# A planner that also places the end pieces of blocks 0 to 3, with block 0's attention first alone

## The chip, the cores and the metric

The program runs on one core of one Trainium2 chip. The metric is the device time of one execution in microseconds, less is better. The kernel before takes 2083.66 us (median of 3 runs, 2082.87 to 2084.57). The engines are named as in the profile: PE (TensorE) with PEld for its weight loads, DVE (VectorE), ACT (ScalarE), POOL (GpSimd) and SP (SyncE, which issues nearly all the DMAs).

## The reference, cut to what matters

Three layers run one after the other on 2304 tokens of width 512: attention with keys and values averaged over groups of 8, a gated layer with 1536 hidden units, and a layer of 8 experts whose mixture matrix is balanced over all tokens in 8 rounds.

```
k_p, v_p = mean over 8 neighbouring rows of k, v          # 576 -> 72 rows
attn = softmax(scale * q @ k_p.T);  x = attn @ v_p        # 4 batches, 8 heads
x2 = (sigmoid(x @ w_gate) * (x @ w_val)) @ w_out          # 512 -> 1536 -> 512
P = exp(x2 @ w_gate2 - max); 8 times: P /= row sums, P /= column sums, P *= N/E
out = sum over e of P[:, e] * (relu(x2 @ w1[e]) @ w2[e])
```

Everything is fp32. A product of the second and third layer is computed as three matmuls on words that were split into a high and a low half (fp32r): high times high, high times low, low times high.

## The kernel before, in words

The tokens are cut into six blocks of 384 (NBLK, numbered 0 to 5), a block into three tiles of 128. The first two layers are done block by block; the experts come afterwards, two blocks (a pair) at a time, from L1157 to the end, and the change doesn't touch them.

Attention of a block j (attend, L925): four k pieces are loaded and summed over 8 on DVE (L266), the v rows are summed on PE by a matmul with a 0/1 matrix (spread_v, L287, batches 0 and 1) or on DVE (L276). For each of three tiles and two head groups, four matmuls give the scores (L309), DVE takes the maxima (L334, or L327 with a subtraction on L328), ACT takes the exponentials, DVE divides by the sum (L359 to L362), PE turns the result (L370, four transposes), ACT copies it, PE multiplies with v (values, L384), ACT rounds the high half of x (L396) and DVE subtracts for the low half (L400). The constant DIRECT says for which blocks ACT takes the exponentials straight from PSUM (j below it), and for which DVE subtracts the maximum first and ACT takes all exponentials at once (L352).

Gated layer: one step is one block and one slice of 128 hidden units. It has the gate product G and the value product V (L226, 12 matmuls of 128x384 each), a sigmoid on ACT (L1028), a multiplication on DVE (L1031), the high half on ACT (L1035), the low half on DVE (L1038), and the output product X (L509). The list steps1 (L107) says in which order steps of blocks 0, 1 and 2 alternate. Weights arrive as 64-bit words and have to be narrowed and split by DVE and ACT before a product can use them (chunk, L843: L162 to L178 and L200 on DVE, L153 and L196 on ACT); a slice has three such chunks.

The order of all this up to the start of block 5 comes from a planner (Plan, L419). Every task has an engine, a key, an assumed duration, the tasks it depends on, and the buffers (room) it takes and frees. The planner plays the engines forward; on each engine the ready task with the lowest key goes next, and the order in which it emits the instructions is the order on the engines' queues, which then wait on semaphores.

A block that has all its 12 slices needs its end pieces (after_block, L560): x2 is split into a high half (ACT, L548) and a low half (L549, a subtraction on POOL for blocks 0 to 4, 128x768), the halves are multiplied with the gate of the experts (12 small matmuls at L226 into "at"), the result is copied (L577), turned (L586) and copied into logits (L589), and the halves are stored. After the second block of a pair there are four more combinations of the two blocks (tt, L599 to L608), each split and stored too. In the planner all this is one generator: from the end of a block on, twelve tasks of the PE queue each run it to its next yield (L1077 to L1083). The planner knows of them only the PE time of the twelve tasks; what they put on ACT, POOL, DVE and SP, and the buffers that they take (the ring of four "fx" tiles, shared with the loads of the wide weights), it doesn't know. Block 5's end pieces run outside the planner, in the first steps of the experts.

Of the kernel before, what the change touches and what calls it, by code (L numbers as in the profile page):

```python
# [21 lines left out]
def attention_moe_moe_kernel(  # L22
# [85 lines left out]
    for j, fs in (  # L108
        (0, (0,)),
        (1, (0, 1)),  # L110
        (0, (1, 2, 3)),
        (1, (2, 3)),
        (2, (0, 1, 2, 3)),
        (1, (4, 5)),
        (0, (4, 5, 6, 7)),
        (1, (6, 7)),
        (2, (4, 5, 6, 7)),
        (1, (8, 9)),
        (0, (8, 9, 10, 11)),
        (1, (10, 11)),  # L120
        (2, (8, 9, 10, 11)),
    ):
        steps1 += [(j, f) for f in fs]
# [112 lines left out]

    class Attention:
# [6 lines left out]
        def load_k(self, b, hp):  # L244
            t = self.krs[b, hp] = self.at.tile([128, SP, POOL], F32, tag="kr", name="kr", bufs=4)
            nc.sync.dma_start(out=t.rearrange("p s j -> p (s j)"), in_=k[b, :, hp * S : (hp + 1) * S])

        def load_v(self, b, i):
            t = self.vrs[b, i] = self.at.tile([128, 2 * DM], F32, tag="vr", name="vr", bufs=4)
            if b >= 2:  # L250
# [12 lines left out]
        def pool_k(self, b, hp):  # L263
            if b not in self.kp:
                self.kp[b] = self.at.tile([128, HP, SP], F32, tag="kp", name="kp", bufs=2)
            nc.vector.tensor_reduce(  # L266
                out=self.kp[b][:, hp], in_=self.krs.pop((b, hp)), axis=AX.X, op=ALU.add
# [55 lines left out]
        def maxima(self, j, t, g):  # L323
            sc = self.pt["s", j, t, g]
            m = self.mx[j, t, g] = self.at.tile([128, 4], F32, tag="mx", name="mx", bufs=6)
            if j >= 2:
# [82 lines left out]
    class Task:  # L409

        def __init__(
            self, key, eng, dur, emit, deps=(), room=None, cond=None, after=None, frees=(), step=-99, size=0
# [3 lines left out]
            self.room, self.cond, self.after, self.frees, self.step, self.size = room, cond, after, frees, step, size  # L416
            self.end = None

    class Plan:  # L419
# [5 lines left out]
        def __init__(self, limits):  # L425
# [5 lines left out]
            self.link = 0.0  # L431

# [12 lines left out]
        def run(self):  # L445
# [10 lines left out]
            while left:  # L456
# [5 lines left out]
                for e, l in queues.items():  # L462
# [12 lines left out]
                    t.emit()  # L475
                    free[e] = now + t.dur
# [303 lines left out]
    with tc.manual_schedule():  # L780
# [59 lines left out]
        OFF = {"g": 0.0, "v": 0.3, "o": 1.0}  # L840
        wide_of = {}

        def chunk(i):  # L843
# [11 lines left out]
            w = add(n - 5, "SP", 0.4, lambda: load_wide(m), room=[("wide", 1)], size=0.524)  # L855
# [16 lines left out]
        def pool(b, key, step):  # L872

            ks = [
                add(key - 3 + 0.01 * i, "SP", 0.45, partial(A.load_k, b, i), room=[("kr", 1)], size=0.295, step=step)
                for i in range(HP)
            ]
            pk = [
                add(
                    key + 0.01 * i, "DVE", 0.72, partial(A.pool_k, b, i), [ks[i]],  # L880
                    room=[("kp", 1)] if i == 0 else None, frees=[("kr", 1)], step=step,
                )
                for i in range(HP)
            ]
            key += V_LATE
            if b < 2:
                vs = [
                    add(
                        key - 3 + 0.01 * i, "SP", 0.8, partial(A.load_v, b, i),
# [5 lines left out]
                for c in range(5):  # L895
                    last = add(
                        key + 0.01 * c, "PE", 0.87,
# [8 lines left out]
            else:  # L906
                vs = [
                    add(key - 3 + 0.01 * i, "SP", 0.55, partial(A.load_v, b, i), room=[("vr", 1)], size=0.295, step=step)
# [11 lines left out]
        V_LATE = 0.3  # L920
        DIRECT = 2
        LEAD = {0: 30.0, 1: 28.0, 2: 6.0, 3: 10.0, 4: 10.0, 5: 10.0}
        ends_in = [((b + 1) * S - 1) // TB for b in range(B)]

        def attend(j):  # L925
# [4 lines left out]
            if j == 1:  # L930
                lo, lead = -24.0, 24.0 + n - 0.5
# [13 lines left out]
            for t in range(TPB):  # L945
                qt = add(at_key(0.0) - 2 + 0.1 * t, "SP", 0.45, partial(A.load_q, j, t), room=[("q", 1)], size=0.262, step=step)
                for g in range(2):
                    key = at_key(0.1 + 0.12 * t + 0.06 * g)
                    s = add(
                        key, "PE", 1.04, with_bank(("s", j, t, g), partial(A.scores, j, t, g)), kps + [qt],  # L950
# [8 lines left out]
                    if j < DIRECT:  # L959
                        es.append(add(key, "ACT", 1.2, partial(A.exps, j, t, g), [m],  # L960
                            frees=gives(("s", j, t, g))
                            + [("kp", 1) for b in range(B) if ends_in[b] == j and (t, g) == (TPB - 1, 1)]))
            if j >= DIRECT:
                x = add(
                    at_key(0.48), "ACT", 4.2, partial(A.softmax, j), ms, step=step,
                    frees=[("kp", 1) for b in range(B) if ends_in[b] == j],
                )
            for t in range(TPB):
# [6 lines left out]
                for g in range(2):  # L975
                    key = at_key(0.64 + 0.1 * t + 0.02 * g)
                    r = add(
                        key, "PE", 0.62, with_bank(("a", j, t, g), partial(A.turn, j, t, g)), [d],
# [10 lines left out]
                    key, "PE", 1.25, with_bank(("x", j, t), partial(A.values, j, t)), cs + vps,  # L989
# [8 lines left out]
        evs = {}  # L998
# [632 lines left out]
```

## Time and profile before

| what | value |
|---|---|
| median of 3 runs | 2083.66 us |
| the profiled execution | 2083.54 us, of which the span of the trace is 2081.8 us |
| PE busy | 2037.4 us, 98% of the span |
| DVE busy | 1259.0 us, 60% |
| ACT busy | 777.5 us, 37% |
| POOL busy | 712.7 us, 34% |
| first product of the gated layer | at 54.57 us |
| first product of the experts | at 595.51 us |

A row of the timeline has the start of a group of equal instructions in us, how long the group lasts, the engine, the line, what it writes and reads, and in brackets how long the engine stood idle before it and what ended that. A row of the windows has a stretch and then, for each engine, its busy time and the number of instructions; PEclk is the granted clock of TensorE, where 1.00 is 2.4 GHz and 0.50 is 1.2 GHz, and a value between is a mixture of the two over the stretch. A matmul's end is modelled, so a busy PE at the lower clock shows as busy all the same.

### The profile page before, as it was taken

The numbers are of one execution on the slowest core, as the hardware profiler recorded it, in microseconds if no ns is written. First come the engines' busy times: TensorE is split into PE (matmuls) and PEld (weight loads), VectorE is DVE, ScalarE is ACT, GpSimd is POOL, SyncE is SP. The second block draws the span as 40 slices with busy tenths as digits, with TensorE's granted clock in tenths as the row PEclk, the third lists the DMA queues.
The fourth block names the chain that finished last, engine by engine and source line by source line (L and its number), as shares of the span: only waits on it lengthen the run. The fifth ranks groups of instructions, "written<-read, shape, count | busy, mean of one in ns | idle before, by whom it ended". The sixth has DMA issues, their size and how long they took to land.

```text
span 2081.8 us, 33236 instructions
## 1 busy us (share of the span) xinstructions
PE 2037.4 (98%) x12721; PEld 1938.8 (93%) x12721; DVE 1259.0 (60%) x2293; ACT 777.5 (37%) x1562; POOL 712.7 (34%) x645
## 2 busy tenths in 40 slices
PE   7999999999989999999999999999999999999998
PEld 5999988988988989888888999999999999999998
DVE  5987944324238786666664656565655656565655
ACT  5543232223233453344333444444443333333332
POOL 0000012001125565445434655665564222222222
PEclk8999999999999999999999999999999999999999
DMA  5677668677966777766769788777889767676764
GB/s 202 230 271 255 221 226 313 214 228 239 374 233 226 290 280 264 258 236 260 260 231 363 277 281 297 282 272 279 297 282 354 288 236 258 243 251 240 252 249 157
DMA packets 171854, 544.83 MB, mean 262 GB/s; under 512 B 15984, under 2 KB 65136, under 8 KB 155312
## 3 DMA queue, kind: packets, MB, share of 16 engines
q1 hardware_dynamic: 171216, 541.14, 72.9%
q8 instruction: 100, 1.64, 0.3%
q0 software_dynamic: 480, 1.57, 0.2%
q14 instruction: 58, 0.48, 0.1%
HBM read 376.72 MB, written 165.94 MB: 261 GB/s over the span
## 4 chain that ended last, share of the span: by engine, by line
PE 92%; DVE 3%; DMA 2%; ACT 1%; issue 1%; POOL 0%; SPq 0%; ACTq 0%; DVEq 0%; POOLq 0%
PE big L1371 22%; PE at L1219 19%; PE gv L1219 14%; PE gv L226 13%; PE big L1250 13%; PE big L509 7%; PE at L309 1%; DMA vr<-in_v_dram 1%; DMA fa<-fad 1%; PE at L384 1%; DVE h L1038 0%; DMA b<-w2d 0%; PE at L370 0%; PE at L226 0%; PE big L287 0%
## 5 line engine op out<-in xcount | busy, mean ns | idle before, releaser
L1310 POOL TENSOR_TENSOR s<-hs,s 128x384 fp32r<-128x384 f32 x192 | 194.9, 1016 | 410.7 <-ACT s L1313 261.0
L226 PE MATMUL gv<-xs,wa 128*128 128x384 f32 x1728 | 322.3, 339 | 2.7 <-DVE xs L400 1.0
L226 PEld LDWEIGHTS gv<-xs,wa 128*128 128x128 f32 x1728 | 301.3, 189 | 7.1 <-issue 1.5
L1250 PE MATMUL big<-w2hl,h 128*128 128x512 f32 x1152 | 296.9, 394 | 0.0
L1353 DVE SCALAR_TENSOR_TENSOR acc<-big,prob,acc 128x256 f32<-128x256 f32 (+1 forms) x462 | 255.2, 584 | 44.6 <-PE big L1371 44.6
L1250 PEld LDWEIGHTS big<-w2hl,h 128*128 128x128 f32 x1152 | 213.8, 188 | 34.3
L1219 PE MATMUL at<-xf,fs 128*128 128x384 f32 x1152 | 237.5, 341 | 1.0 <-ACT c L1422 0.6
L1219 PE MATMUL gv<-xf,fs 128*128 128x384 f32 x1152 | 234.0, 338 | 1.8 <-DVE a L1300 1.8
L1219 PE MATMUL at<-xf,fa 128*128 128x384 f32 x1152 | 228.0, 337 | 3.0 <-DMA fa<-fad 1.2
L1219 PEld LDWEIGHTS at<-xf,fa 128*128 128x128 f32 x1152 | 198.4, 188 | 9.6 <-DVE c L1549 1.6
L1219 PEld LDWEIGHTS gv<-xf,fs 128*128 128x128 f32 x1152 | 198.5, 189 | 7.4 <-DVE a L1300 2.1
L1219 PEld LDWEIGHTS at<-xf,fs 128*128 128x128 f32 x1152 | 198.4, 190 | 5.2 <-ACT c L1422 1.0
L509 PE MATMUL big<-h,wa 128*128 128x384 f32 x864 | 168.6, 341 | 10.1 <-ACT h L1035 4.9
L509 PEld LDWEIGHTS big<-h,wa 128*128 128x128 f32 x864 | 152.3, 190 | 14.7 <-DVE h L1038 8.2
L1371 PE MATMUL big<-t,s 128*128 128x256 f32 x1152 | 162.8, 282 | 0.8 <-DVE acc L1353 0.8
L1371 PE MATMUL big<-b,a 128*128 128x256 f32 x1152 | 158.5, 282 | 1.9 <-DVE a L1300 1.9
L1371 PEld LDWEIGHTS big<-t,s 128*128 128x128 f32 x1152 | 157.1, 189 | 1.0 <-DVE acc L1353 1.0
L1371 PEld LDWEIGHTS big<-b,a 128*128 128x128 f32 x1152 | 153.5, 189 | 2.4 <-DVE a L1300 2.3
L1435 DVE TENSOR_TENSOR gv<-gv,c 128x384 f32<-128x384 f32 x64 | 36.2, 566 | 197.1 <-PE gv L1219 193.6
L549 POOL TENSOR_TENSOR fx<-x,fx 128x768 fp32r<-128x768 f32 x10 | 18.6, 1872 | 394.3 <-ACT fx L548 393.5
L1279 DVE SCALAR_TENSOR_TENSOR acc<-big,prob,acc 128x512 f32<-128x512 f32 x144 | 107.5, 747 | 70.9 <-PE big L1250 68.9
L1313 ACT ACTIVATE s<-hs 128x384 fp32r<-128x384 f32 x192 | 100.5, 524 | 110.6 <-DVE hs L1306 110.6
(176 smaller groups left out, 3079.2 us busy)
## 6 DMA issues: line engine op xcount, KB each, us to landing
wa<-words SPq DMA_DIRECT2D x144, 512.0 KB, 4.4
fs<-fsd SPq DMA_DIRECT2D x64, 1024.0 KB, 7.3
fa<-fad SPq DMA_DIRECT2D x64, 768.0 KB, 4.8
b<-w2d SPq DMA_DIRECT2D x192, 256.0 KB, 5.8
raw<-in_moe_w_dram SPq DMA_DIRECT2D x64, 512.0 KB, 7.1
fsd<-fs SPq DMA_DIRECT2D x32, 1024.0 KB, 5.5
w2d<-w2hl SPq DMA_DIRECT2D x32, 1024.0 KB, 4.4
fad<-fa SPq DMA_DIRECT2D x32, 768.0 KB, 5.4
```

The source lines that it names most:

```text
L226: nc.tensor.matmul(out=out_, lhsT=a[s], rhs=b[m], start=(i == 0), stop=(i == n - 1))
L309: nc.tensor.matmul(out=sc[c0:c1, i], lhsT=self.qs[j, t][pr, i, c0:c1], rhs=self.kp[b][pr, i], start=True, stop=True,)
L384: nc.tensor.matmul(out=po[pr, h // 2, c0:c1], lhsT=self.vp[b][:, h * D : (h + 1) * D], rhs=a[:, 4 * (h % 2) + h // 2, c0:c1], start=True, ...
L509: nc.tensor.matmul(out=x2p[d][:, :TB], lhsT=w[s][:, d * 128 : (d + 1) * 128], rhs=gs[j, f][m], start=(first and i == 0), stop=(last and i ...
L1219: nc.tensor.matmul(out=pt[:, :TB], lhsT=w[:, s, i, k], rhs=t[:, o, k], start=(start and m == 0), stop=(m == 5), skip_group_check=True,)
L1250: nc.tensor.matmul(out=py, lhsT=h[:, s, cs], rhs=w2hl[n][:, o, fh], start=(m == 0), stop=(m == 5))
L1279: nc.vector.scalar_tensor_tensor(out=acc[t], in0=py, scalar=pr, in1=acc[t], op0=ALU.mult, op1=ALU.add)
L1310: nc.gpsimd.tensor_tensor(out=t[:, 1], in0=x, in1=f32(t[:, 0]), op=ALU.subtract)
L1313: nc.scalar.activation(out=t[:, 0], in_=x, func=AF.Copy)
L1353: nc.vector.scalar_tensor_tensor(out=o, in0=src, scalar=pr, in1=o, op0=ALU.mult, op1=ALU.add)
L1371: nc.tensor.matmul(out=o, lhsT=hp[n0 + k, h][:, s, i * 128 : (i + 1) * 128], rhs=pieces2[n0, w][:, k, b], start=(first and m == 0), stop=( ...
L1435: nc.vector.tensor_tensor(out=vc, in0=vc, in1=c2, op=ALU.add)
```

## The change

Six things change in the code.

1. The end pieces of blocks 0 to 3 become planner tasks of their own (settle), each with engine, duration and room: a rounding on ACT, a subtraction on DVE (no longer POOL), a store, the small matmuls, the copy, the turn. The twelve tasks that ran the generator go. Block 4's and 5's end pieces keep the old way.
2. steps1 begins with two slices of block 0, then four of block 1, then two of block 0.
3. Block 1's attention starts at the key START = -5.5 (before: -24) and runs to one step before the step of its first product.
4. The loads at the start get keys from a table (FETCH): k and q of block 0, the gate weights, v of block 0, then the other weights, then block 1's.
5. DIRECT becomes 3, so block 2's exponentials are taken by ACT straight from PSUM. The planner adds 1.28 to an ACT task that changes the table of functions, and some durations have two values, before the first step and after it.
6. Blocks 2 to 5 start their attention further ahead (LEAD).

KROWS is 0, so the new spread_k and keep_k, which it would switch on, put no instruction into the program.

```diff
     for j, fs in (
-        (0, (0,)),
-        (1, (0, 1)),
-        (0, (1, 2, 3)),
-        (1, (2, 3)),
+        (0, (0, 1)),
+        (1, (0, 1, 2, 3)),
+        (0, (2, 3)),
         (2, (0, 1, 2, 3)),
...
+    DIRECT = 3
+    KROWS = 0
+    VROWS = 2
...
                     t.emit()
+                    if isinstance(t.dur, tuple):
+                        t.dur = t.dur[self.at_step >= 0]
+                    if t.table and t.table != self.table:
+                        self.table = t.table
+                        t.dur += 1.28
...
-        OFF = {"g": 0.0, "v": 0.3, "o": 1.0}
+        FETCH = {
+            ("w", 0): -31.0,
+            ("k", 0): -39.0,
...
+        OFF = {"g": 0.0, "v": 0.5, "o": 1.0}
...
-        V_LATE = 0.3
-        DIRECT = 2
-        LEAD = {0: 30.0, 1: 28.0, 2: 6.0, 3: 10.0, 4: 10.0, 5: 10.0}
+        V_LATE = 4.3
+        START = -5.5
+        LEAD = {0: 30.0, 1: 28.0, 2: 9.0, 3: 27.0, 4: 14.0, 5: 20.0}
...
             if j == 1:
-                lo, lead = -24.0, 24.0 + n - 0.5
+                lo, lead = START, n - 1.0 - START
...
             if f == NF1 - 1:
-                t = X
-                for k in range(12):
-                    t = add(
-                        n + 1.6 + k, "PE", 2.2 if k == 2 else 0.05, lambda: next(gate, None), [t],
-                        step=n + 1 + k,
-                    )
+                settle(j, n + 1.0, keeps)
             return X
+
+        def settle(j, key, keeps):
...
+            def halves(name, src, deps, store):
...
+                a = add(tick(), "ACT", 0.84, high, deps, room=[("wide", 1)])
+                b = add(tick(), "DVE", 0.95, low, [a])
...
+                return b, add(
+                    tick(), "SP", 0.4, lambda: fx_store(fx[name], p, store), [b], size=0.79, frees=[("wide", 1)]
+                )
...
+            a = add(
+                tick(), "PE", 2.1, with_bank(("l", j), sums), [l0, l1], cond=free_tag,
+                frees=[("wide", 1)] if odd else (),
+            )
...
+            d1 = add(tick(), "DVE", 0.95, sub(0, half(1, 0), half(0, 0)), [*keeps, b], room=[("wide", 1)])
+            d2 = add(tick(), "DVE", 0.95, sub(1, half(1, 1), tt(0)), [d1])
+            l1, _ = halves("t1", tt(0), [d1], 3)
+            l2, _ = halves("t2", tt(1), [d2], 4)
```

What the new keys do to the queues is seen in the order of the instructions. On PE, the program before begins with these rows (L287 sums v, L309 is one group of scores for every x4):

```order
L287 MATMUL at<-vr,spread 72x512 x3
L309 MATMUL at<-kp,qt 128x72 x4
L287 MATMUL at<-vr,spread 72x512
L309 MATMUL big<-kp,qt 128x72 x4
L287 MATMUL at<-vr,spread 72x512
L309 MATMUL at<-kp,qt 128x72 x4
```

The program of the change begins on PE with these (L341 are the scores, L319 sums v, L402 turns):

```order
L341 MATMUL at<-kp,qt 128x72 x8
L341 MATMUL big<-kp,qt 128x72 x12
L319 MATMUL at<-vr,spread 72x512
L341 MATMUL at<-kp,qt 128x72 x4
L319 MATMUL at<-vr,spread 72x512
L402 MATMUL big<-ident,e 72x128 x4
```

Five groups of scores now stand ahead of the first sum of v, where three sums of v stood ahead of the first scores.

The second place is PE around the first product. Before, the last turns and values of blocks 0 and 1 (L370, L384) stand directly ahead of it:

```order
L370 MATMUL at<-ident,e 72x128 x4
L384 MATMUL big<-a,vp 64x128 x8
L370 MATMUL at<-ident,e 72x128 x4
L384 MATMUL at<-a,vp 64x128 x8
L226 MATMUL gv<-xs_581,wa 128x384
```

In the change three groups of values of block 1 and one turn come behind it (L416 are the values; the 64x64 form is the tile with two batches; xs_491 and xs_492 are the two halves of block 0's x):

```order
L416 MATMUL at<-a,vp 64x128 x8
L225 MATMUL gv<-xs_491,wa 128x384
L225 MATMUL gv<-xs_492,wa 128x384
L225 MATMUL gv<-xs_491,wa 128x384 x2
L225 MATMUL gv<-xs_492,wa 128x384
L225 MATMUL gv<-xs_491,wa 128x384 x2
L225 MATMUL gv<-xs_492,wa 128x384
L225 MATMUL gv<-xs_491,wa 128x384 x2
L225 MATMUL gv<-xs_492,wa 128x384
L225 MATMUL gv<-xs_491,wa 128x384
L416 MATMUL at<-a,vp 64x64 x16
L402 MATMUL at<-ident,e 72x128 x4
```

All six score groups of block 1, five of its six turns and its sums of v still stand ahead of the first product, and so does one score group of block 2.

The third place is the end pieces. Before, POOL has these rows between its setup and the weights of the experts (x_0 is x2 of block 0, tt a combination of two blocks):

```order
L549 TENSOR_TENSOR fx<-x_0_822,fx 128x768 x2
L549 TENSOR_TENSOR fx<-x_1_966,fx 128x768 x2
L549 TENSOR_TENSOR fx<-tt,fx 128x768 x4
L549 TENSOR_TENSOR fx<-x_2_1689,fx 128x768 x2
L549 TENSOR_TENSOR fx<-x_3_4180,fx 128x768 x2
L549 TENSOR_TENSOR fx<-tt,fx 128x768 x4
L549 TENSOR_TENSOR fx<-x_4_5015,fx 128x768 x2
```

In the change POOL keeps the last of these rows alone, and the other 16 subtractions stand on DVE (L1165) between the g and h operations of the steps (L1101 and L1108, which were L1031 and L1038); here is the place of block 0's last and block 1's two:

```order
L1165 TENSOR_TENSOR fx<-x_0_924,fx 128x768
L1101 TENSOR_TENSOR g<-g,gv 128x384
L1108 TENSOR_TENSOR h_3048<-g,h_3047 128x384
L569 TENSOR_TENSOR x_1_1339<-x_1_1339,big 128x384 x4
L1101 TENSOR_TENSOR g<-g,gv 128x384
L1165 TENSOR_TENSOR fx<-x_1_1339,fx 128x768 x2
L1108 TENSOR_TENSOR h_3114<-g,h_3113 128x384
```

Two of the subtractions now stand in a row between a step's multiplication and its low half.

## Rows read from the trace of the kernel before

**Rows 1.** The page, busy time of the engines.
```profile
PE 2037.4 (98%) x12721; PEld 1938.8 (93%) x12721; DVE 1259.0 (60%) x2293; ACT 777.5 (37%) x1562; POOL 712.7 (34%) x645
```
**Rows 2.** Windows of the ramp; PEclk is the granted clock.
```profile
20.00:30.00 10.00, 10.00 (x36) 6.60 (x35) 6.20 (x20) 5.74 (x37) 0.00 (x0) 0.55 0.59 188
30.00:40.00 10.00, 9.49 (x63) 5.48 (x62) 7.02 (x19) 6.81 (x28) 0.00 (x0) 0.77 0.17 54
40.00:50.00 10.00, 9.26 (x99) 7.67 (x99) 8.48 (x20) 8.37 (x35) 0.00 (x0) 0.83 0.29 107
```
**Rows 3.** Timeline, start of the ramp: start us, us, engine, line.
```profile
7.87 0.75 DVE L266 TENSOR_REDUCE kp<-kr 128x72 f32<-128x576 f32 x1 [1.87 <-DMA kr<-in_k_dram]
8.71 5.37 PE L287 MATMUL at<-vr,spread 128*72 128x512 f32 x6 [8.71 <-DMA vr<-in_v_dram]
14.01 1.14 PE L309 MATMUL at<-kp,qt 64*128 64x72 f32 x8
...
22.72 1.98 PE L309 MATMUL at<-kp,qt 64*128 64x72 f32 x8
```
**Rows 4.** Timeline of PE, end of the ramp.
```profile
50.67 0.63 PE L370 MATMUL at<-ident,e 128*72 128x128 f32 x4
51.23 1.09 PE L384 MATMUL big<-a,vp 72*64 72x128 f32 x16
...
54.57 4.43 PE L226 MATMUL gv<-xs,wa 128*128 128x384 f32 x24
```
**Rows 5.** Timeline of PE among the first steps.
```profile
67.87 1.11 PE L309 MATMUL at<-kp,qt 64*128 64x72 f32 x8
68.91 2.35 PE L509 MATMUL big<-h,wa 128*128 128x384 f32 x12
```
**Rows 6.** Timeline of ACT: an exponential, a table load, block 2's softmax.
```profile
15.95 0.32 ACT L341 ACTIVATE e<-at,mx 128x72 f32<-128x72 f32 x1 [13.65 <-DVE mx L335]
...
94.86 1.28 ACT L352 ACT_TABLE_LOAD   x1
...
96.16 1.65 ACT L352 ACTIVATE e<-e 128x1728 f32<-128x1728 f32 x1
```
**Rows 7.** Timeline of PE where block 2 joins.
```profile
121.20 0.45 PE L226 MATMUL gv<-xs,wa 128*128 128x384 f32 x1 [0.69 <-ACT xs L396]
...
122.64 7.92 PE L226 MATMUL gv<-xs,wa 128*128 128x384 f32 x35 [1.00 <-DVE xs L400]
```
**Rows 8.** Waits of PE, 240 to 600 us: total, times, longest.
```profile
PE big L509 <- ACT h L1035: 4.9, 4, 1.7
PE big L509 <- DVE h L1038: 4.7, 7, 1.2
PE at L586 <- DVE lt L577: 1.5, 2, 0.7
PE at L370 <- DVE e L362: 1.0, 1, 1.0
```
**Rows 9.** Windows of three stretches with the lower clock.
```profile
120.00:130.00 10.00, 8.32 (x42) 7.81 (x39) 6.74 (x13) 3.47 (x6) 0.00 (x0) 0.83 0.61 209
331.50:335.00 3.50, 3.50 (x13) 3.50 (x13) 0.00 (x0) 0.84 (x1) 1.73 (x2) 0.51 1.01 407
348.60:352.00 3.40, 3.32 (x10) 3.32 (x11) 0.85 (x3) 0.00 (x0) 0.00 (x0) 0.50 1.02 422
```
**Rows 10.** Timeline around an end piece on POOL, and later without one.
```profile
327.21 0.96 DVE L607 TENSOR_TENSOR tt<-x,tt 128x768 f32<-128x768 f32 x1 [2.41 <-POOL fx L549]
...
500.67 1.83 POOL L549 TENSOR_TENSOR fx<-tt,fx 128x768 fp32r<-128x768 f32 x1 [21.30 <-ACT fx L548]
...
501.03 1.88 DVE L1038 TENSOR_TENSOR h<-g,h 128x384 fp32r<-128x384 f32 x1 [1.65 <-ACT h L1035]
...
502.97 2.20 PE L509 MATMUL big<-h,wa 128*128 128x384 f32 x11 [1.02 <-DVE h L1038]
...
519.37 0.56 DVE L1038 TENSOR_TENSOR h<-g,h 128x384 fp32r<-128x384 f32 x1 [0.59 <-ACT h L1035]
```

More of the change, by code (lines that the diff above doesn't have):

```diff
@@ L411, in __init__ @@
         def __init__(
-            self, key, eng, dur, emit, deps=(), room=None, cond=None, after=None, frees=(), step=-99, size=0
+            self, key, eng, dur, emit, deps=(), room=None, cond=None, after=None, frees=(), step=-99, size=0,
+            table=None,
         ):
@@ L431, in __init__ @@
             self.link = 0.0
+            self.table = None
         def add(self, *a, **kw):
@@ L872, in pool @@
         def pool(b, key, step):
[L874 to L881, printed above, removed]
-                )
-                for i in range(HP)
-            ]
+            if b < KROWS:
+                ks = [
+                    add(
+                        FETCH["k", b] + 0.01 * c, "SP", 0.45, partial(A.load_k, b, c),
+                        room=[("kr", 1)], size=0.262 if c < 4 else 0.131, step=step,
+                    )
+                    for c in range(5)
+                ]
+                last = None
+                for c in range(5):
+                    last = add(
+                        key + 0.01 * c, "PE", (0.8, 0.5),
+                        with_bank(("k", b), partial(A.spread_k, b, c)) if c == 0
+                        else partial(A.spread_k, b, c, None),
+                        [ks[c], last], cond=free_tag if c == 0 else None,
+                        room=[("kp", 1)] if c == 0 else None,
+                        frees=[("kr", 1)], step=step,
+                    )
+                pk = [add(key, "ACT", 0.4, partial(A.keep_k, b), [last], frees=gives(("k", b)), step=step)]
+            else:
+                ks = [
+                    add(FETCH.get(("k", b), key - 3) + 0.01 * i, "SP", 0.45, partial(A.load_k, b, i), room=[("kr", 1)], size=0.295, step=step)
+                    for i in range(HP)
+                ]
+                pk = [
+                    add(
+                        key + 0.01 * i, "DVE", 0.72, partial(A.pool_k, b, i), [ks[i]],
+                        room=[("kp", 1)] if i == 0 else None, frees=[("kr", 1)], step=step,
+                    )
+                    for i in range(HP)
+                ]
@@ L907, in pool @@
                 vs = [
-                    add(key - 3 + 0.01 * i, "SP", 0.55, partial(A.load_v, b, i), room=[("vr", 1)], size=0.295, step=step)
+                    add(FETCH.get(("v", b), key - 3) + 0.01 * i, "SP", 0.55, partial(A.load_v, b, i), room=[("vr", 1)], size=0.295, step=step)
                     for i in range(4)
@@ L945, in attend @@
             for t in range(TPB):
-                qt = add(at_key(0.0) - 2 + 0.1 * t, "SP", 0.45, partial(A.load_q, j, t), room=[("q", 1)], size=0.262, step=step)
+                qt = add(FETCH.get(("q", j), at_key(0.0) - 2) + 0.1 * t, "SP", 0.45, partial(A.load_q, j, t), room=[("q", 1)], size=0.262, step=step)
                 for g in range(2):
@@ L964, in attend @@
                 x = add(
-                    at_key(0.48), "ACT", 4.2, partial(A.softmax, j), ms, step=step,
+                    at_key(0.48), "ACT", 1.65, partial(A.softmax, j), ms, step=step, table="exp",
                     frees=[("kp", 1) for b in range(B) if ends_in[b] == j],
@@ L997, in attention_moe_moe_kernel @@
         gate = iter(())
-        evs = {}
         open_ = {}
@@ L1044, in products @@
             prev_g[0] = G
-            SG = add(n + 0.2, "ACT", 0.49, sigmoid, [G], room=[("g", 1)], frees=[("gv", 1)])
+            SG = add(n + 0.2, "ACT", 0.49, sigmoid, [G], table="sig", room=[("g", 1)], frees=[("gv", 1)])
             V = add(
```

137 lines of the change are left out of this document (119 added, 18 removed).

## Prediction

> **What bounds the kernel now.** I began with the busy times [rows 1]: PE is busy for 98% of the span and no other engine for more than 60%, so time can come from three things alone: PE standing idle, PE at the lower of its clocks, and PE's start. The total work of PE is the same in both programs (the same products, scores, turns, values and sums of v). So I looked for PE's lost time in the part that the planner orders, up to 595 us; what follows is ordered by code that is not touched.
>
> The ramp comes first. PE gets its first work at 8.71 us, and its first product of the gated layer at 54.57 us [rows 3, 4]. The windows between show PE busy 9.3 to 10 of 10 us, so it hardly waits there; what it loses is clock: 0.55, 0.77 and 0.83 granted in the three windows from 20 to 50 us [rows 2]. Since the granted clock is either 2.4 or 1.2 GHz, those are (1 - 0.55)/0.5 x 10 = 9.0 us, 4.6 us and 3.4 us at the lower one, 17.0 us in all, and half of that, 8.5 us, is lost. The same group of scores shows it: 1.14 us at 14.01, 1.98 us at 22.72 [rows 3].
>
> Next, the place at which block 2 joins: its first product waits 0.69 us for the high half of the last tile of x, and 1.00 us for the low half [rows 7]; the clock falls behind it to 0.83 over 10 us, 3.4 us at the lower one [rows 9], so 1.7 us more. Together 3.4 us.
>
> Last, the waits of PE from 240 to 600 us [rows 8]: 4.9 + 4.7 us for the two halves of h, 1.5 us for the copied logits, 1.0 us for e, 12.1 us in all; and two stretches at the lower clock of 3.5 and 3.4 us [rows 9], half of which is 3.4 us. Together 15.5 us. How the end pieces make these waits is seen in one of them [rows 10]: a subtraction of the end pieces runs on POOL from 500.67 for 1.83 us, the low half of h on DVE begins beside it and takes 1.88 us instead of 0.56, and X waits 1.02 us. At 327.21 DVE itself had waited 2.41 us for POOL to have read tt.
>
> So 8.5 + 3.4 + 15.5 = 27.4 us can be had at most from rows that show a loss.
>
> **The change part by part.** The ramp (other loads, block 0 alone first, block 1 later). Scores now lead PE's queue, and the fourth k piece is summed at 7.87 + 0.75 = 8.62 us [rows 3], so PE starts at about 8.7 us as before, on scores instead of sums of v. Ahead of the first product three groups of values and one turn are gone, at 1.09 us each and 50.67 to 51.23 = 0.56 us [rows 4], and one score group of block 2 is new, 67.87 to 68.91 = 1.04 us [rows 5]: 3.27 + 0.56 - 1.04 = 2.8 us less. This is not a gain, since PE does it behind the first product. At the pace of before the first product comes at 54.57 - 2.8 = 51.8 us and the ramp is worth nothing. Only a better clock or fewer waits make it worth something: upwards all 8.5 us; downwards the five leading score groups at 1.98 instead of 1.14 us [rows 3], 4.2 us lost. I take 2 us gained, near nothing, because the row that this is nearest to is the half-clock stretch from 20 us, in which PE was kept busy with the same mixture of scores and sums of v that now follows the five groups; the 2 us are for the exponentials' chain, which starts 14.01 - 8.71 = 5.3 us earlier. First product at about 50 us.
>
> A rule of the Trainium skill bears on the clock (TensorE: Matmul & The Clock Gate, section What's actually happening): the lower clock is the default and activity releases it. The trace disagrees for this work: from 20 to 30 us PE shows 10.00 of 10 us busy at 0.55. By the rule the busy ramp would run at 2.4 GHz, and the sum would have 8.5 us here instead of 2; that is the first rival below.
>
> DIRECT and steps1. Block 2's scores cost ACT six groups of four exponentials at 0.32 us, 7.7 us, in place of one of 1.65 us, and two more table loads of 1.28 us [rows 6]: 8.6 us more on ACT between the first product and block 2's, which lay 67 us apart before (54.57 and 121.20, [rows 4, 7]). I cost this at nothing, with ACT's idle time as the cover (it is busy for 37% of the span, [rows 1]); if the cover is gone it is 8.6 us (the rival on the other side). DVE is freed of the subtractions and sums of that block, which helps the weights' chain; I take nothing for it.
>
> Where block 2 joins, its longer lead (9 steps instead of 6) puts, in the order of the change, one product and one X between the last values and block 2's first product, 2 x 2.2 us (a product or an X has 12 matmuls, and 24 take 4.43 us, [rows 4]), where before the waits for the halves of x were 0.69 and 1.00 us. So the wait goes, and the fall of the clock behind it should: 3.4 us at most, 0 at least. I take 3. What is late next there is the weights' chain on DVE.
>
> The end pieces. Gone from POOL are 16 subtractions of 1.83 us; DVE gets 16 of 0.95 us (priced by its own subtraction of the same 128x768 shape at 327.21, 0.96 us [rows 10]), 15 us in 360 us in which it has much room. The collisions of POOL with h go, the waits for tt behind POOL go, and the copied logits get one product as cover before PE turns them. What stays is DVE's order: in one place two subtractions stand in a row between a step's multiplication and its low half, 1.9 us, while the row at 519.37 shows that the low half otherwise follows within 0.6 us of the multiplication's end by way of ACT; PE then covers this with the next product of 2.2 us or waits up to 1 us. With all 15.5 us gone as the upper bound, and 6 us as the lower (the clock stretches 3.4, the logits' 1.5 and e's 1.0 go, every wait for h stays as it was), I take 13, nearer to the upper one, because the 4.7 us behind DVE are waits of about 1 us of the kind in rows 10, and those had a POOL subtraction beside them.
>
> A rule against this step is in the Trainium skill (Perfetto Trace Analysis, section Optimizing Scalar/DVE Operations): work moved between GpSimd and DVE may not help, since they share a read port. The 1.88 against 0.56 us [rows 10] shows the sharing, but as the loss that the move ends. By the rule the 4.7 us of waits for DVE's h would stay, and the sum would be 4.7 us worse.
>
> The sum: 2 + 3 + 13 = 18 us, off the profiled execution's 2083.54 us (0.1 us under the median of the runs): 2065.5, so 2065 us.
>
> **The rivals.**
> - The ramp runs at the full clock. For it: once the first products run, the clock stays up; against it: rows 2. Then 8.5 + 3.4 + 15.5 = 27.4 us, 2056 us.
> - The waits move to DVE. For it: the end pieces now stand in DVE's queue between a step's multiplication and its low half, and a 0.95 us piece there is as long as the waits of rows 8. Then the end pieces give their lower bound 6, the join 2, the ramp 0: 2075.5 us. Against it: the planner now knows of these pieces and their time.
> - No change that can be measured: the end pieces' 6 us are given back in a ramp at the lower clock throughout (-4.2) and the join brings 0: 2082 us.
> - Slower, by ACT. Exponentials and table loads of block 2 stand in ACT's queue ahead of sigmoids and of the roundings that the weights wait for. If all 8.6 us come in front of products, and the ramp loses its 4.2 us, the join 0, the end pieces 6: 2083.5 + 8.6 + 4.2 - 6 = 2090 us. It decides as soon as ACT has less idle time between the first product and block 2's than those 8.6 us; the windows of the ramp show ACT at 5.7 to 8.4 of 10 us [rows 2], and it falls behind that.
>
> That the change does not do what it says is excluded: the order shows the 16 subtractions on DVE and block 1's values behind the first product.
>
> **How the numbers follow.** The forecast 0.55 (own range 2058 to 2071), the full clock 0.20, waits on DVE 0.17, no change 0.04, slower 0.04. What a measurement of this kernel can tell from no change is 0.2%, 4.2 us. The first three lie beyond it: faster 0.92, same 0.04, slower 0.04. From 2056 less what a run may scatter to 2076 holds all but the last two and the rims: 2053 to 2077.
>
> **What would show it.** Right: the first product near 50 us with block 1's values behind it; no wait in front of block 2's first product; from 240 us on no DVE h above 0.7 us, PE's waits there down from 12 us to 3 or less, and no stretch at the lower clock; the first product of the experts at about 595.5 - 18 = 577 us, and the time behind it as long as before. Wrong: a first product at 54 us or later, waits of products for DVE's or ACT's splitting of the weights between 55 and 110 us, or X waiting for h behind DVE's subtractions.

## The result, and the profile after

The kernel after takes 2057.53 us (median of 4 runs, 2051.49 to 2061.21), beside 2083.26 us for the kernel before on the same chip: 25.7 us less, a ratio of 0.9873, 95% interval 0.9848 to 0.9898. The forecast was 2065 us with a range of 2053 to 2077. The profiled execution is the fastest of the four, 2051.49 us with a span of 2049.8 us, so 32.0 us lie between the two traces and 25.7 between the medians. One of the four executions of run 9 below, the profiled one, had a granted clock of 0.555 from beginning to end and took 3312.95 us, so the median of run 9 is taken over the other three and its trace isn't set beside the others.

Where the 32.0 us lie is read from four points of PE's timeline in each trace:

| stretch of PE | before, us | after, us | difference |
|---|---|---|---|
| up to its first work | 8.71 | 7.58 | -1.13 |
| first work to first product | 45.86 | 35.83 | -10.03 |
| first product to first product of the experts | 540.94 | 518.15 | -22.79 |
| the rest, up to the end of the span | 1486.29 | 1488.24 | +1.95 |

The page's busy line, which answers to [rows 1]:

```profile
PE 2021.3 (99%) x12721; PEld 1930.4 (94%) x12721; DVE 1257.1 (61%) x2302; ACT 786.3 (38%) x1611; POOL 682.5 (33%) x629
```

POOL has lost 30.2 us, nearly all of it the 16 subtractions, and ACT has got 8.8 us, block 2's exponentials and the table loads. DVE is where it was: it took over the subtractions of the end pieces, but block 2's own subtractions went with DIRECT (7.4 us, by the pages of the kernel after and of run 11), and its low halves of h became shorter (below).

The windows of the ramp, which answer to [rows 2]. The columns are the same: the stretch, then PE, PEld, DVE, ACT, POOL, then PEclk.

```profile
10.00:20.00 10.00, 10.00 (x43) 6.63 (x42) 7.56 (x24) 7.62 (x49) 0.00 (x0) 1.00 1.05 363
20.00:30.00 10.00, 9.26 (x73) 5.86 (x71) 8.55 (x16) 6.42 (x12) 0.00 (x0) 1.00 0.88 323
30.00:40.00 10.00, 10.00 (x94) 7.49 (x93) 9.45 (x29) 9.18 (x54) 0.00 (x0) 1.00 0.35 105
40.00:50.00 10.00, 9.66 (x85) 7.08 (x83) 9.58 (x18) 8.47 (x21) 0.00 (x0) 1.00 0.66 231
```

PEclk is 1.00 in all four, where it was 0.55, 0.77 and 0.83 in the last three. The timeline of PE in the ramp answers to [rows 3 to 5]:

```profile
7.58 2.24 PE L341 MATMUL at<-kp,qt 64*128 64x72 f32 x13 [7.58 <-DMA qt<-in_q_dram]
...
16.99 1.98 PE L319 MATMUL at<-vr,spread 128*72 128x512 f32 x2
...
22.05 1.02 PE L319 MATMUL at<-vr,spread 128*72 128x512 f32 x2
...
43.41 2.36 PE L225 MATMUL gv<-xs,wa 128*128 128x384 f32 x12
45.69 1.09 PE L416 MATMUL at<-a,vp 72*64 72x128 f32 x16
46.72 2.37 PE L225 MATMUL gv<-xs,wa 128*128 128x384 f32 x12
49.02 1.20 PE L416 MATMUL at<-a,vp 72*64 72x64 f32 x32
```

The first product comes at 43.41 us and block 1's values stand behind it (two of the three groups are shown). A pair of sums of v takes 1.98 us at 16.99 and 1.02 us at 22.05: up to about 21.8 us PE runs at half its speed, from then on at its full one, although the column of the granted clock has 1.00 for both.

Behind the ramp, the windows from 60 us to the end of the blocks, first of the kernel before, then of the kernel after:

```profile
60.00:240.00 180.00, 177.36 (x1051) 173.14 (x1050) 154.22 (x287) 74.31 (x133) 0.00 (x0) 0.99 0.74 258
240.00:560.00 320.00, 306.90 (x1888) 285.79 (x1887) 126.75 (x223) 83.74 (x140) 36.54 (x22) 0.99 0.74 253
```

```profile
60.00:240.00 180.00, 180.00 (x1096) 175.05 (x1095) 158.28 (x301) 81.58 (x164) 0.00 (x0) 1.00 0.68 250
240.00:560.00 320.00, 319.86 (x1985) 305.91 (x1984) 119.33 (x213) 84.23 (x144) 13.78 (x13) 1.00 0.81 284
```

PE stood idle for 2.6 and 13.1 us before, and for 0.0 and 0.1 us after. No row of a wait is left that could answer to [rows 7, 8], and in place of the first window of [rows 9] there is PEclk 1.00 over 120 to 130 us. The first product of the experts:

```profile
561.56 1.20 PE L1381 MATMUL at<-xf,fa 128*128 128x384 f32 x6
```

### The profile page after: what moved, and what is told of

Its sections match the earlier page's. It is cut to its first block, busy times and chain, and to the rows that moved or that the text cites. A ratio compares the mean times of both kernels' runs of the same rounds, so it can differ in the third digit from the quotient of the medians.

```text
span 2049.8 us, 33256 instructions
## 1 busy us (share of the span) xinstructions
PE 2021.3 (99%) x12721; PEld 1930.4 (94%) x12721; DVE 1257.1 (61%) x2302; ACT 786.3 (38%) x1611; POOL 682.5 (33%) x629
## 4 chain that ended last, share of the span: by engine, by line
PE 93%; DMA 4%; DVE 1%; ACT 1%; issue 0%; POOL 0%; SPq 0%; DVEq 0%; ACTq 0%
PE big L1533 22%; PE at L1381 19%; PE gv L225 14%; PE gv L1381 14%; PE big L1412 12%; PE big L549 7%; PE at L341 1%; DMA b<-w2d 1%; PE at L416 1%; PE at L402 1%; DMA xf<-xd 1%; DMA vr<-in_v_dram 1%; DMA fa<-fad 1%; ACT e L373 0%; PE at L319 0%
## 5 line engine op out<-in xcount | busy, mean ns | idle before, releaser
L589 POOL TENSOR_TENSOR fx<-x,fx 128x768 fp32r<-128x768 f32 x2 | 3.7, 1846 | 492.6 <-ACT fx L588 489.4
L549 PE MATMUL big<-h,wa 128*128 128x384 f32 x864 | 162.2, 335 | 0.0
```

The costliest lines, as they stand in the source:

```text
L549: nc.tensor.matmul(out=x2p[d][:, :TB], lhsT=w[s][:, d * 128 : (d + 1) * 128], rhs=gs[j, f][m], start=(first and i == 0), stop=(last and i ...
```

## The experiments

Times are medians. The kernel before, measured beside them, took 2083.35 us with runs 1 to 4, 2084.3 with runs 5 to 8 and 2084.1 with runs 9 to 12; gains are against these.

**1. The kernel after once more** (no edit).

> The changed kernel once more, to see what its runs scatter with. Theory A (the clock of the ramp differs from execution to execution): runs between 2050 and 2062 us; each run's time less (1 - granted clock) x span is the same within 3 us, and the profile of a slower run shows stretches at the lower clock before the first product. Theory B (the runs differ in waits, by DMA or between engines): the clock is the same in all runs and the profile of a slower run shows waits of PE of several us.

2057.28 us (2052.49 to 2059.35), ratio 0.9873, 0.9858 to 0.9889. The profiled execution is one of 2059.35 us, and its windows of the ramp show what the other did not:

```profile
20.00:30.00 10.00, 9.27 (x88) 6.42 (x87) 9.67 (x20) 6.67 (x13) 0.00 (x0) 1.00 0.86 313
30.00:40.00 10.00, 10.00 (x61) 7.67 (x58) 7.14 (x20) 7.98 (x49) 0.00 (x0) 0.50 0.33 106
40.00:50.00 10.00, 9.70 (x41) 5.98 (x41) 6.86 (x15) 6.18 (x18) 0.00 (x0) 0.82 0.33 119
```

The same instructions in the same order run at half the clock from 29.8 to 43.5 us, and the first product comes at 48.76 us. From there to the experts the two traces are alike (517.94 and 518.15 us). So 5.35 of the 7.86 us between the two executions are the clock of the ramp; the rest lies behind the first product of the experts, where this trace has three short stretches at the lower clock (at 576, 586 and 1098 us) and the other has one (at 571). That is theory A in the main: each run's time less what the granted clock cost it agrees within 3.7 us, where the theory said 3.

**2. The end pieces alone** (before, with settle in place of the generator):

```diff
...
-                t = X
-                for k in range(12):
-                    t = add(
-                        n + 1.6 + k, "PE", 2.2 if k == 2 else 0.05, lambda: next(gate, None), [t],
-                        step=n + 1 + k,
-                    )
+                settle(j, n + 1.0, keeps)
...
```

> The kernel before with the planned end pieces alone (settle, subtractions on DVE); start, steps1, DIRECT, LEAD and durations as before. Theory A (the gain behind 240 us comes from the end pieces alone): first product at 54.5 us as before, the waits of PE from 240 to 595 us fall from 12.6 us to under 2 us, no stretch at the lower clock there, 2083.3 - 17 = 2066 us. Theory B (the longer LEAD of blocks 2 to 5 does half of it, by moving attention out of the end pieces' way): about 6 us of waits stay, 2074 us.

2063.76 us, ratio 0.9909 (0.9893 to 0.9926), 19.6 us less. Its windows:

```profile
60.00:240.00 180.00, 177.35 (x1052) 172.89 (x1051) 153.49 (x286) 73.38 (x132) 0.00 (x0) 0.99 0.73 259
240.00:560.00 320.00, 320.00 (x2012) 304.92 (x2012) 136.04 (x247) 90.09 (x150) 8.36 (x7) 1.00 0.77 275
```

Up to 240 us it is the kernel before, with the same 2.6 us of waits; from 240 us on PE never stands idle, as theory A said. That is more than the 15.5 us which the prediction gave as the most that the end pieces could bring.

**3. The rest alone** (after, with the old generator and POOL in place of settle; the leads, the start and DIRECT stay new):

```diff
-                settle(j, n + 1.0, keeps)
+                t = X
+                for k in range(12):
...
```

> The changed kernel with the end pieces as before (the generator of twelve PE tasks, subtractions on POOL); all else changed. Theory A: first product between 43 and 52 us as the clock of the ramp falls, no wait where block 2 joins, X waits for h of about 10 us from 240 us on as before: 2083.3 - 3 (join) - 2 to 9 (ramp) = 2071 to 2078 us. Theory B (LEAD does half of the later gain): waits of about 6 us behind 240 us, 2066 to 2072 us.

2062.18 us, ratio 0.9898 (0.9884 to 0.9913), 21.2 us less: neither theory had so much. The waits of PE from 60 to 565 us:

```profile
PE big L549 <- ACT h L1105: 2.3, 2, 1.7
PE at L626 <- DVE lt L617: 1.4, 2, 0.7
PE big L549 <- DVE h L1108: 0.3, 2, 0.2
```

With the old end pieces on POOL 4.0 us of waits are left of the 13.1. So something else in the change takes away more than two thirds of what was put down to the end pieces, and 19.6 and 21.2 us can't be added.

**4. The planned end pieces on POOL** (after, with the 16 subtractions back on POOL and their time in the planner):

```diff
-                    nc.vector.tensor_tensor(
+                    nc.gpsimd.tensor_tensor(
...
-                b = add(tick(), "DVE", 0.95, low, [a])
+                b = add(tick(), "POOL", 1.85, low, [a])
```

> The changed kernel with the 16 subtractions of the planned end pieces on POOL, with 1.85 us as the planner's duration for them. Theory A (what the planner knows is the larger part, the collisions of POOL with DVE the smaller): operations of DVE that run beside POOL take 1.9 us again, 16 times at most, but PE waits under 6 us from 240 us on: 3 to 5 us slower than the changed kernel, 2061 us. Theory B (the collisions are nearly all of it): PE's waits behind 240 us come back to 10 us or more, 2068 us or slower. Theory C (planned, the collisions cost nothing): within 1 us of the changed kernel.

2054.61 us, ratio 0.9865 (0.9850 to 0.9879), not to be told from the kernel after. The collision of [rows 10] is still there, at other places, here in the timeline of POOL and DVE and then of PE:

```profile
278.99 3.65 POOL L1165 TENSOR_TENSOR fx<-x,fx 128x768 fp32r<-128x768 f32 x2 [9.61 <-ACT fx L1162]
279.75 0.55 DVE L1101 TENSOR_TENSOR g<-g,gv 128x384 f32<-128x384 f32 x1 [2.04 <-ACT fx L1162]
...
280.90 2.16 DVE L1108 TENSOR_TENSOR h<-g,h 128x384 fp32r<-128x384 f32 x1 [0.59 <-ACT h L1105]
...
281.57 2.26 PE L225 MATMUL gv<-xs,wa 128*128 128x384 f32 x12
283.67 2.24 PE L549 MATMUL big<-h,wa 128*128 128x384 f32 x12
```

The low half takes 2.16 us beside POOL's subtraction, where its mean in the kernel after is 0.55, and ends at 283.06. X doesn't wait for it, since until 283.67 PE has the logits' small products and one product to do; in [rows 10] X stood right behind a product that began at 499.42. Over all steps h takes as long here as before (rows of the groups by line, DVE, 57 to 560 us, first before, then this kernel, then the kernel after):

```profile
L1038 DVE TENSOR_TENSOR h<-g,h 128x384 fp32r<-128x384 f32 x60 | 38.7, 646 | 14.9 <-ACT h L1035 14.9
```

```profile
L1108 DVE TENSOR_TENSOR h<-g,h 128x384 fp32r<-128x384 f32 x59 | 37.7, 639 | 14.5 <-ACT h L1105 14.5
```

```profile
L1108 DVE TENSOR_TENSOR h<-g,h 128x384 fp32r<-128x384 f32 x59 | 32.6, 553 | 10.1 <-ACT h L1105 10.1
```

A mean of 639 ns against 646, and PE waits 0.3 us for it instead of 4.7:

```profile
PE big L549 <- DVE h L1108: 0.3, 1, 0.3
```

So the slow subtraction beside POOL does not cause the loss by itself: here work of PE lies between it and X, in [rows 10] none does.

**5 and 6. Four matmuls ahead of all other work of PE**, in the kernel after and in the kernel before, on a tile of ones, their result unused:

```diff
...
+        nc.vector.memset(warm_src, 1.0)
...
+        for _ in range(4):
+            nc.tensor.matmul(out=warm_pt, lhsT=warm_src[:, :128], rhs=warm_src, start=True, stop=True)
```

> The kernel after, with four matmuls of 128x512 on a tile of ones put ahead of all other work of PE; their result is not used. Theory A (what differs between the runs of the kernel after, 2051.5 to 2061 us, is PE's granted clock before and just behind the first product: at the lower clock until 21.8 us in the fastest run, and again from 29.8 to 43.5 us in the run of 2059.35 us): with PE busy from a few us on, the clock rises earlier, the stretch of 13.7 us does not come back, first product near 40 us, 2045 to 2052 us, and the runs lie within 3 us of each other. Rival B (the lower clock does not depend on what PE did before the first scores): the rows of the ramp are as in the kernel after, the median stays at 2057 us or grows by what the four matmuls delay the first scores, up to 3 us, 2057 to 2060 us, with the same scatter.

> The kernel before, with the same four matmuls ahead of PE's work. In the kernel before 8.5 us are lost to the lower clock from 20 to 50 us. Theory A (early work of PE brings the clock up): the first product comes near 46 to 50 us instead of 54.6, and the time is 2075 to 2080 us. Rival B (the mixture of scores and sums of v itself keeps the clock down, since PE was busy there 10.00 of 10 us at 0.55): first product at 54 to 57 us, 2083 to 2086 us.

In the kernel after 2054.84 us, ratio 0.9861 (0.9847 to 0.9874), not to be told from it without them; in the kernel before 2084.65 us, ratio 0.9995 (0.9986 to 1.0004). The timeline and the windows of the kernel after with them:

```profile
1.66 5.56 PE L828 MATMUL big<-warm_src 128*128 128x512 f32 x8 [1.66 <-DVE warm_src L825]
7.74 1.25 PE L341 MATMUL at<-kp,qt 64*128 64x72 f32 x13 [0.51 <-DVE kp L274]
```

```profile
20.00:30.00 10.00, 9.06 (x96) 7.84 (x96) 9.45 (x22) 6.71 (x30) 0.00 (x0) 0.80 1.03 373
30.00:40.00 10.00, 10.00 (x44) 6.99 (x43) 6.60 (x19) 5.75 (x30) 0.00 (x0) 0.50 0.21 65
40.00:50.00 10.00, 10.00 (x52) 6.12 (x51) 6.79 (x12) 6.79 (x19) 0.00 (x0) 0.85 0.53 193
```

The first half of theory A holds: 13 scores take 1.25 us instead of 2.24, and the ramp is ahead. The second half fails: the clock falls at about 26 us to one half until 43 us, with PE busy all the while, and the first product comes at 46.01 us, between 43.41 and 48.76. In the kernel before the lower clock stays where it was too (0.50 from 20 to 30 us); its first product comes at 52.42 us, between the two theories, and its time is the one of rival B. What PE did earlier doesn't keep the clock up in this ramp. The runs of the kernel after lie within 2.2 us of each other with them and within 9.7 without, but runs 4 and 12 lie within 2.7 and 2.2 without them too, so the four matmuls are not shown to do that.

**7. The start alone, with the old leads** (run 3 with this edit more):

```diff
-        LEAD = {0: 30.0, 1: 28.0, 2: 9.0, 3: 27.0, 4: 14.0, 5: 20.0}
+        LEAD = {0: 30.0, 1: 28.0, 2: 6.0, 3: 10.0, 4: 10.0, 5: 10.0}
```

> The kernel after with the old end pieces (generator, subtractions on POOL) and with the old leads of blocks 2 to 5 (6, 10, 10, 10); what is left of the change is the order of the start: loads, steps1, block 1's attention, DIRECT. The run with the new leads (start only) took 2062.2 us and waits only 4 us from 240 us on. Theory D (the longer leads took away the waits among the end pieces, since x of the next block is ready sooner and the planner has more work to place between): the waits from 240 us on come back to 9 to 13 us, 2069 to 2075 us. Rival E (the other order of steps and of the start did it, by moving the end pieces against h): the waits stay at 4 to 6 us, 2061 to 2065 us.

2070.58 us, ratio 0.9937 (0.9923 to 0.9950), 13.7 us less.

```profile
60.00:240.00 180.00, 179.22 (x1074) 174.99 (x1075) 148.46 (x285) 83.14 (x182) 0.00 (x0) 1.00 0.70 249
240.00:560.00 320.00, 309.47 (x1918) 290.04 (x1917) 121.78 (x208) 84.74 (x142) 37.94 (x23) 0.99 0.79 271
```

```profile
PE big L549 <- DVE h L1108: 4.2, 8, 1.0
PE big L549 <- ACT h L1105: 3.8, 3, 1.7
```

10.5 us of waits from 240 us on, 4.2 of them for DVE's h and 3.8 for ACT's: theory D. The join of block 2 loses its wait by the start alone.

**8. The leads alone** (before, with the new leads):

```diff
-        LEAD = {0: 30.0, 1: 28.0, 2: 6.0, 3: 10.0, 4: 10.0, 5: 10.0}
+        LEAD = {0: 30.0, 1: 28.0, 2: 9.0, 3: 27.0, 4: 14.0, 5: 20.0}
```

> The kernel before with the new leads of blocks 2 to 5 (9, 27, 14, 20) and nothing else. Theory D (the leads alone take away most waits behind block 2's joining and among the end pieces): no wait where block 2 joins, 3 to 6 us of waits from 240 us on instead of 12, 2068 to 2074 us. Rival E (the leads do nothing without the other order): waits from 240 us on 10 us or more, 2079 to 2084 us.

2066.33 us, ratio 0.9916 (0.9903 to 0.9930), 18.0 us less by four numbers, and a little more than theory D had.

```profile
60.00:240.00 180.00, 179.76 (x1093) 174.75 (x1094) 165.31 (x311) 79.46 (x140) 0.00 (x0) 1.00 0.71 253
240.00:560.00 320.00, 314.52 (x1933) 297.97 (x1932) 109.96 (x202) 81.83 (x140) 38.21 (x23) 0.99 0.80 276
```

The join's wait is gone, and of 13.1 us from 240 us on 5.5 are left, with the end pieces as they were.

**9. End pieces and leads, with the old start** (run 2 with the edit of run 8).

> The kernel before with the planned end pieces and the longer leads, and with the old start (loads, steps1, block 1 early, DIRECT 2). End pieces alone gave 19.6 us, leads alone 18.0, the two of the start and the leads 21.2. Theory F (end pieces and leads take away the same waits of PE, which can go only once; what is left is the ramp): no wait from 60 us on above 0.5 us in all, first product at 52 to 55 us, 2061 to 2065 us, so that the order of the start is worth 4 to 8 us in the kernel after. Rival G (they take away different waits): 19.6 + 18.0 us less, 2047 us, or at least as fast as the kernel after, 2057 us or less.

2058.3 us, ratio 0.9875 (0.9859 to 0.9892), 25.8 us less. The median is taken over three runs, 2056.95 to 2058.49, and there is no trace to be read with the others. Neither theory had this value. The two don't add up, as F said, but the order of the start is then worth nothing that can be measured, where F said 4 to 8: the kernel after gained 25.7 us, and 26.1 in run 1. The intervals allow for about 5 us either way.

**10. POOL and the four matmuls** (the edits of runs 4 and 5 together).

> The kernel after with the 16 subtractions on POOL (2054.6 alone) and the four matmuls ahead of PE's work (2054.8 alone). If each of the two takes 2.5 us by a way of its own, 2050 to 2053 us; if both differ from the kernel after only by the clock that the runs happened to get in the ramp, 2054 to 2058 us.

2053.41 us (2050.25 to 2054.36), ratio 0.9851 (0.9837 to 0.9866), between the two expectations, with the lower clock from about 24 to 41 us again and the first product at 46.17. Its interval overlaps that of the kernel after: that it is a better version is not shown.

**11. DIRECT = 2** in the kernel after:

```diff
-    DIRECT = 3
+    DIRECT = 2
```

> The kernel after with DIRECT = 2, so that block 2's maxima are subtracted on DVE again and ACT takes one exponential of 1.65 us instead of six groups. Theory of the prediction (ACT's 8.6 us lie beside other work and cost nothing): 2054 to 2060 us, and ACT busy 8 us less. Rival, ACT's work was in the way: 2048 to 2053 us. Rival, DVE's relief was needed for the weights: waits of products for the weights' halves between 55 and 120 us, 2061 to 2068 us.

2054.83 us, ratio 0.9862 (0.9843 to 0.9880), not to be told from the kernel after. The page has ACT at 777.7 us, 8.6 less than with DIRECT = 3. That is the work that the prediction had counted, and no cost of it can be measured, nor any gain.

**12. Block 1's attention early** in the kernel after:

```diff
-        START = -5.5
+        START = -24.0
```

> The kernel after with START = -24, so that block 1's attention is ahead of the first product again, as in the kernel before; about 5 us of PE work go back ahead of it. Theory H (the work is only moved: the ramp is worth what the clock grants): first product at 48 to 53 us, no new waits, 2053 to 2061 us as the kernel after. Rival I (the gain of the ramp comes from spreading block 1's attention between products): 2062 to 2068 us, with a longer stretch at the lower clock ahead of the first product.

2053.58 us (2051.9 to 2054.08), ratio 0.9856 (0.9839 to 0.9872). The first product comes at 48.11 us with more work ahead of it, and the first one of the experts at 561.75, as in the fastest run of the kernel after: theory H, the work is only moved.

## Why the prediction came out as it did

The direction and the order of size were right, 18 us forecast and 25.7 measured. The levers of the change taken apart:

| what is new | gain, us | idle of PE 60 to 240 us | 240 to 560 us |
|---|---|---|---|
| start (7) | 13.7 | 0.8 | 10.5 |
| leads (8) | 18.0 | 0.2 | 5.5 |
| end pieces (2) | 19.6 | 2.6 | 0.0 |
| start and leads (3) | 21.2 | 0.0 | 3.9 |
| end pieces and leads (9) | 25.8 | no trace | no trace |
| all (kernel after) | 25.7 | 0.0 | 0.1 |

**The sum of 3 and 13 us for the join and the end pieces is the step that was off, by its size.** Run 9, with the old start, has 25.8 us where it had 16, and the end pieces alone brought 19.6 against an upper bound of 15.5. The mechanism was there: no wait is left, and the clock no longer falls at 123, 331 and 348 us. What the bound missed can be read from the traces. From the first product to the experts 22.79 us went although about 2.8 us of work had been moved in, so 25.6 us. The windows of this stretch, first before, then after:

```profile
54.57:595.51 540.94, 524.89 (x3168) 499.25 (x3168) 293.11 (x531) 169.50 (x293) 43.78 (x29) 0.99 0.73 253
```

```profile
43.41:561.56 518.15, 518.01 (x3229) 497.55 (x3228) 292.68 (x541) 179.78 (x339) 13.78 (x13) 1.00 0.76 269
```

PE stood idle for 16.1 us of it before and for 0.1 after: 15.9 us, where the bounds of the prediction held 13.8, since the waits for g, a and some halves of h were not among its rows. The clock is the prediction's 5.1 us. That makes 21.0 and leaves 4.6 us, in which PE shows as busy. They fit the price of a wait. The place of [rows 10] again, PE of the kernel before:

```profile
499.42 2.35 PE L226 MATMUL gv<-xs,wa 128*128 128x384 f32 x12
501.61 0.34 PE L509 MATMUL big<-h,wa 128*128 128x384 f32 x1
502.97 2.20 PE L509 MATMUL big<-h,wa 128*128 128x384 f32 x11 [1.02 <-DVE h L1038]
505.10 1.09 PE L384 MATMUL at<-a,vp 72*64 72x128 f32 x16
```

and, in the same trace, an X without a wait between the same two neighbours:

```profile
394.23 2.35 PE L226 MATMUL gv<-xs,wa 128*128 128x384 f32 x12
396.42 2.24 PE L509 MATMUL big<-h,wa 128*128 128x384 f32 x12
398.60 1.09 PE L384 MATMUL at<-a,vp 72*64 72x128 f32 x16
```

From its start to the start of what follows X takes 505.10 - 501.61 = 3.49 us with the wait and 398.60 - 396.42 = 2.18 us without. The wait is shown as 1.02 us of idle time and costs 1.31. The first matmul shows 0.34 us by itself, while 12 in a row follow each other every 0.18 us: consecutive matmuls overlap, and at a wait the overlap is lost. The other three X of this kind in the kernel before, with waits of 0.22, 0.76 and 1.02 us, cost 0.52, 1.05 and 1.31, each 0.3 us more than their idle time. The waits of the stretch are 21 in number, so an estimate from these four is 6 us for all of them, of the size of the 4.6 that are left; that every wait costs so much was not measured.

**The leads were costed at the join alone.** Four numbers brought 18.0 us, nearly as much as the end pieces. The prediction gave them 3. In run 8 POOL's subtractions and the twelve generator tasks are unchanged, and yet the waits from 240 us on fall from 13.1 to 5.5. End pieces and leads take away largely the same waits, and the start some of them; each alone looks like nearly the whole gain. Which of its two effects the lead works by, more PE tasks to put between h and X or the end pieces lying against other steps, was not separated.

**The collision with POOL does not suffice as the cause.** The prediction moved near its upper bound because "those had a POOL subtraction beside them". Run 4 keeps the subtractions on POOL and the long h, and the waits are gone all the same. The leads alone decide much of it: with the pieces unplanned and on POOL, PE waits 4.2 us for DVE's h with the old leads (run 7) and 0.3 with the new ones (run 3); with the old start it is 4.7 and 1.7 (the kernel before and run 8). What the planner's knowledge of the pieces does by itself was not separated from the move to DVE, since no run has planned pieces on POOL with the old leads. The rule of the Trainium skill that was weighed there (Perfetto Trace Analysis, section Optimizing Scalar/DVE Operations), that GpSimd and DVE share a read port and moving work between them may not help, agrees with run 4 in the time: with the new leads no difference between the two engines can be measured. The 4.7 us by which the rule was said to make the sum worse did not come: no X waits for DVE's h in the kernel after.

**The ramp**, 2 us taken, between -4.2 and 8.5. In the profiled run the first product came 11.16 us earlier, less 2.8 us moved, 8.4 us: the size of the first rival, but not on its ground, since the ramp did not run at the full clock. Up to about 21.8 us PE works at half its speed, which costs (21.8 - 7.58)/2 = 7.1 us. The kernel before had such a stretch too, where the granted clock also shows 1.00 and which the prediction passed over: its first six sums of v take 5.37 us [rows 3], while with the four matmuls ahead (run 6) the same six take 2.77:

```profile
8.14 2.77 PE L287 MATMUL at<-vr,spread 128*72 128x512 f32 x6 [0.83 <-DMA vr<-in_v_dram]
```

So the kernel before lost 2.6 us there on top of the 8.5, and by the clock the ramp gained 8.5 + 2.6 - 7.1 = 4.0 us. PE started 1.1 us earlier and stood idle 1.3 us less (2.35 and 1.08 us from its first work to its first product); 2.0 us are not explained. In run 1 the same program had 5.35 us less. The lower bound happened as well: five score groups do run at half speed at the head of the queue. In the medians the start adds nothing that can be measured on top of end pieces and leads, by the first products nearer 5 (45.6 us in the mean of the six traces with the new start and nothing ahead of it or moved in it, 53.7 in the three with the old, 2.8 moved); which of the two holds is open, because there is no trace of run 9 to set beside the others. The rule that activity releases the clock (the Trainium skill, TensorE: Matmul & The Clock Gate, section What's actually happening) fits the four matmuls of run 5, after which the first scores ran at full speed, and not the windows of runs 1 and 5, in which PE is busy 10.00 of 10 us at 0.50.

**What was right.** Block 1's values stand behind the first product and are only moved (run 12). ACT's 8.6 us cost nothing that can be measured (run 11), and PE is busy for 180.00 of 180 us where the rival on the other side had it wait. The waits did not move to DVE: h takes 553 ns in the mean, 646 before, and no X waits for it (a single one takes 0.74 us, where the prediction allowed 0.7). The time of the experts grew by 1.95 us where it was said to stay; over the thirteen traces that can be set side by side it lies between 1486.3 and 1491.0 us, and the kernel before has the lowest of these. The clock doesn't explain the 1.95: the lower one costs 3.4 us there before (1123 to 1131 us) and 1.7 after (571.4 to 574.8).

## What to carry to other kernels

An edit to the lead of a pipelined stage and an edit to how side work is planned can remove the same waits; when two parts of a change have one loss to remove, price the loss once and not each part by the place at which it stands in the code. A wait of PE costs more than its idle time in the trace: count from the start of the waiting product to the start of what follows, and compare with a product between the same neighbours that doesn't wait. A slow instruction beside another engine's work matters only if nothing lies between it and its reader, so look there before moving it to another engine.

## What the runs showed of the hardware

The clock of the ramp isn't fixed by the program: the kernel after got 1.00 over 30 to 40 us in one run and 0.50 in another, and its eight runs spread from 2051.5 to 2061.2 us. The old start spreads too: the kernel before took 2081.67 to 2087.52 us in the fifteen runs beside runs 5 to 8. The PEclk column shows 1.00 for the first 20 us of the kernel after, although the matmuls there take twice as long as later (1.98 against 1.02 us): at the very start the durations are the better witness.
